# Where the value copies of layer B read from: SBUF row by row, or a copy in DRAM, two features at a time

## The chip, the cores and the metric

The kernel runs on one core of one Trainium2 chip. Its time is the device time of one execution in microseconds (us), without the host. The core has five engines that work side by side and meet only at semaphores: TensorE (PE, matmuls, with its weight loads shown apart as PEld), VectorE (DVE), ScalarE (ACT), GpSimd (POOL) and SyncE (SP), which here issues nearly all DMAs. Each engine runs its own list of instructions in order.

## The reference

The input x is 2048 rows of 512 features. Four layers run one after the other, A, B, A, B, each added to its input:

```
x = x + A(layernorm(x)); x = x + B(layernorm(x)); x = x + A(layernorm(x)); x = x + B(layernorm(x))
```

Layer A is a linear attention of 32 heads of 16 features: two softmaxes of each projected query and key, a sum over all rows that makes one small matrix per head, and a quotient. Every row of its second part needs the sum over all 2048 rows.

Layer B is an attention over a short window: row s looks at rows s, s-2, ..., s-14 of the same head, eight in all.

```
idx = pos[:, None] - (jnp.arange(8) * 2)[None, :]          # rows before 0 are masked
logits = einsum("bhsd,bhswd->bhsw", q, k[idx]) * Dh ** -0.5
attn = softmax(logits, axis=-1)
o = einsum("bhsw,bhswd->bhsd", attn, v[idx])
return o.reshape(B, S, D) @ wo
```

## The kernel before

**Blocks.** The 2048 rows are cut into four blocks of 512, b = 0 to 3, and L = 0 or 1 says which of the two A-B pairs is meant. A stage of a block is a closure registered under a name: `a1` to `a4` are layer A (keys and values, queries, denominators, output), `b1` projects queries, keys and values of layer B, `b2` makes the logits and the softmax, `b3` applies the weights to the values. `akv0` and `akv1` are the two places where the sum over all rows is turned into the matrices that `a3` and `a4` use.

**Two forms of layer B.** Seven of the eight blocks of layer B are elementwise: DVE multiplies shifted copies (`prod` at L1043, `pav` at L1105, four of each per block, a tile of 128 x 4096), and PE sums them with 0/1 matrices (`lgt` at L1050, `mo` at L1114). The eighth, L = 1 and b = 3 (`EST`), is done on PE with masked scores (`sc` at L1278, `b3_13.mo` at L1322, 128 short instructions each, four of them) and has its own way through DRAM (tile `Vs`, `vd`, the copies into `WA` and `Vx`, the copies `Qbd`).

**The values.** In an elementwise block the values V lie in one tile of 128 partitions by 4 x 528 elements: partition 4h + dl holds head h and feature dl of each of the four groups of features. The multiplication by the weights needs each feature dl on the partitions of all 32 heads and four window pairs g: `Vg[k]` with k = dl // 2 is a tile of [128, 2, 2112] in which partitions 32g to 32g + 31 hold the row of feature dl, shifted by 2g elements. The step `vrep(dl)` makes it with four DMAs, one for each g in the order 0, 2, 1, 3; each reads 32 partitions of V with a stride of four and writes 32 partitions, 4208 bytes a row. A block needs sixteen of them. `pav(q)` reads `Vg[q // 2]`, so the first two multiplications of a block need the first eight copies and the last two need the other eight.

**The order.** Nothing is scheduled on the chip. `_ORDER` lists all steps in the order in which they are recorded; an engine gets its own steps in that order. `_CHOICE` says for each flexible step (a copy out of PSUM, a normalization, a residual) whether ACT or DVE does it. `_SLOTS` says which of the fixed buffers each new tile takes: `ps` are the eight PSUM banks, `big` the eight large buffers in which `Ek`, `prod`, `pav`, `Vg`, `Qbd` and `Vx` follow one another, `med` and `t2` smaller ones. A step that takes a buffer waits for the last reader of its earlier tile. SP takes its DMAs in order too: a DMA that waits at the head of SP's list holds back all behind it, among them the transposes `xnT` (L473) that feed the next layer, the copies `Prho` (L855) of layer A and the stores of the result (L567).

**Steps that the prediction names.** `ev(2, c)` of `b1` are the four copies of V out of PSUM (tile `V`, L205 on ACT, L203 on DVE); `vhalo_in` (L989, POOL) fills the first sixteen columns of V; `vwr` (L997) writes V to DRAM and stands in the program before only behind an option that is off; `ld_raw1` are the two loads of raw key weights at the start (tile `wraw`, L349).

Of the kernel before, what the change touches and what calls it, by code (L numbers as in the profile page):

```python
# [19 lines left out]
H = 32  # L20
# [28 lines left out]
    "v_dram": (),  # L49
# [12 lines left out]
8 2e a d c 23 i i i 0 j 9 k j l i 2 i i i i 0 b o p i f 2 0 1m 1m 1o m n i i i i 1n 1m 1m 1p 1q 1m 1r o q r 1m t  # L62
4 z 1s s z i 3 1t 1u 21 z z 10 3 1t i7 1v 22 22 21 1 24 24 2p z 0 t u 13 11 15 1t 1t t 16 1w 1t 1y 12 12 12 12
1x x 1t 5 v w w 25 y 14 2f 2f 18 18 18 18 1z 2g 2c 17 6 19 18 1c 1d 39 2d 1b 1a 2d 22 22 1f 1f g 21 22 22 3a 3a
2c 2c 1f 2d 20 21 1f 22 2c 7 7 20 20 22 26 29 1g 1f 1k 39 3a 2d 2d 2d 2d 1i h 3b 2f 24 2i 1h 1e 29 1j 1l 2q 2h
27 2d 2n 3c 2o 2o 29 29 2a 39 2k 2k 3a 2k 2k 2n 2n 2n 2q 2o 2o 2r 3a 3a 2q 2q 2o 2o 2o 29 2y 2y 2l 2s 2k 2o 2z
2z 2z 2z 31 31 36 3c 33 24 36 36 28 36 2y 2y 2v 2v 2z 2v 37 36 2z 2z 2z 2f 2j 2u 2v 2b 2w 2b 2b 2b 2m 36 2m 36
2m 36 36 2m 39 3a 3b 3b 31 2v 2t 3a 31 32 4e 37 3c 34 35 39 3a 2x 2x 3c 2x 30 2x 38 38 36 38 38 3i 3c 3b 3c 3c
3c 7 3d 3e 3e 3j 3k 3k 3b 3k 3c 3l 5h 3m 3n 3m 3d 3e 3d 3l 5i 3o 3m 3e 3e 3l 3p 3m 3q 3r 3m 3m 5j 3d 3v 5i 3e 3e
3s 3e 20 20 20 20 3t 3m 5h 3u 5n 3m 3m 5m 3d 3e 7c 5h 5q 5o 5p 5r 5k 5i 3f 3g 3g 7 3f 3g 3g 5l 3m 5i 5i 7d 3w 3x  # L70
5i 5i 3z 5i 5i 3f 3f 7e 5i 5s 3g 3y 3g 40 41 7d 5w 42 7f 41 41 7f 41 5t 7f 3g 5v 3g 5u 5x 44 43 45 bd 43 43 46
43 47 5y 3f 43 47 48 90 5x 5x 4b e 49 4c 60 61 41 41 4a 41 41 3g 5x 5z 5z 4d 4g 4g 4h 5z 62 5z 4l 4l 4l 91 92 7d
7d 7g 63 4i 5z 91 4f 4n 4q 4q 4m 4q 63 66 67 64 65 7j 7i 7h 4l 7k 4r 93 4g 4g 4j 4w 4w 7l 7l 4o 4w 7o 68 4k 4q
4u 93 93 4t 4s 4f 7l 7p 7m 7n 4p 4v 7n 7l 7q 6p 6k 6k 4v 6k 7n 7n 91 91 6f 6g 7r 6n 6m 6k 6a 6a 4w 94 6l 7n 69
7r 7u 6o 7v 96 7t 97 4x 95 7s 7w 98 4x 4x 4x 6f 6c 6h 4y 4y 6a 6d 6b 6r 6r 99 6f 6i 6r 99 3h 99 99 9d 9e 3h 6f
6j 6a 6e 9a 9b 9c 9b 6r 9b 9b 83 7y 7y 84 9f 9b 8d 7z 6s 6s 6s 9f 9h 6s 6t 6t 88 89 9i 7y 6s 6t 4w 4x 83 83 6q
6q 7y 6q 85 88 4y 88 8b 83 9g 87 86 81 b2 9j 9k 88 8c 9m 9n 8f 9w 9x 82 9w 9w a1 6r 9z 69 6u 9w 80 6u 6v 8a 6u
6v 6x 6v 4w 6w 6q 6u 6v 6y 9m 4v 4z 4z 6z 4v 70 71 4z 4z 70 70 9y 72 7x 73 72 74 70 75 72 72 76 9o 9r 9r 50 51
8f 50 50 72 52 76 78 8e 8e 50 53 77 54 9r 9u 79 7a 9m 9p 7b 8f 9s 9t 55 8e 56 57 8f 55 58 55 55 59 8g 8g 8g 8e
a0 8g 57 57 a3 9r 5a 57 9v 9m 9q 5b a3 57 5b 8h 8h 5c b3 5e 5d 5f 5g 7x 9l a2 b0 b0 a3 b1 b1 b1 8g 8h b1 b3 b3  # L80
b6 b3 b7 bz c0 c0 a4 a4 a4 a3 a4 a5 a5 bz c0 c0 bz d3 b4 bz c0 c0 c0 c0 8f 8i b0 b1 a4 8i 8i 8i a5 as at b0 b1
b1 bx ap a2 b5 b1 ap 8j 8k 8j 8j 8l 8m 8j bx 8n 8o a3 a6 a2 a6 8p 8o 8o 8o bx aq aq aq aq by by by 8q 8t 8r 8s
as 8q a2 as as bx a6 a7 8q 8q a7 by 8u bz 8q a6 8u 8w 8y by by aw av 8v a7 8x a8 a7 aa ap ap a9 ab ac b8 b8 au
ac i7 ac ac by by bx b8 b8 ad aq aq af aq aq ag b9 bo c0 8z ah b8 bb bb ae ae ae ae ai be ax ae ai aj an c1 be
bc bb bc bc ak ax bc bb bc bc bc bc ac ac am ax ac ax ay al ac bg be bm bm ao bm bm bj bn bn bn bn bn bn ar ax
# [12 lines left out]
ig gs gs gs if if ig ig gp du if ig gs gt gt gt gt if gu ig if du du gu du dv ic c5 ic ic fd ih fe ih ih dy ig
ih ic dz ic dw ii ii fi ij gr gr gt ij ik ij ij fj fj ik il ga gu il in gs fl ii ij ij gv ii fj fj im ij ij ik
il ik fn fo gr gr il gw gx iq io iq iq gv gw gv gw gv gv ip iq iv dx dx fk fm fm gy gz h2 is gw gw ir it h2 iw  # L100
iu h0 it ix iw h3 h3 h4 h5 h6 h2 h1 h3 h7 h2 h5 h3 h8 h5 h5
# [4 lines left out]
    "0010110111100111111111000000100000100110011100000111011110010100000101010000100000000000111101011100"  # L106
    "1010010100001100100000000000000011111110000100001010100000000000000000010111001000001101000000000000"
    "1010000011111100000000000100010110011011010100101111000000001001000000010110010001000100011100100000"
    "00000000011111010000011100000000000000000000000001000011001000000000000000001100"
)  # L110


_SLOTS = {
    "med": (
        "0123456789abcdef346aff72ffc3105f92b4de6a7fd92b317ef99962c0517dbf2e3abf6925cd13e273a31dad901d74235cdb"
        "f72a94d35c017b9264acf31d08"
    ),
    "ps": (
        "0123124350123021456715604156734153267234701623047237452365001230210345672135304675261473045672350146"
        "1401230453013042567103651251741023452036714302310345031240230435406703203501467012012457245201240310"  # L120
        "3245602750235102563740130473024567142362047540123640760437034563745101021345067241301456701236204531"
# [8 lines left out]
        "333333301045234102"  # L130
    ),
    "pp": (
        "640620202020"
    ),
}


class _Fast:
# [804 lines left out]
    def s_b1(self, L, b):  # L943
# [55 lines left out]
        def vrep(dl):  # L999
            if dl == 0:  # L1000
                self.Vg[L, b] = {}
# [1099 lines left out]
```

## Time and profile before

| what | us |
|---|---|
| median of 3 runs (lowest, highest) | 328.83 (328.43, 328.86) |
| the profiled execution | 329.39 |
| its span, first to last instruction | 327.7 |
| PE / DVE / ACT busy in the span | 308.8 / 296.3 / 278.1 |

The span is what the trace covers; the profiled execution took 1.7 us more than it, and 0.6 us more than the median. Three engines are busy for 85 to 94% of the span. PE's figure holds overlaps, since the ends of matmuls are modelled. "issue" among the causes of a wait is time in which the engine waited for nothing that the profile shows. A row of the timeline gives start, length and count of merged instructions, and in brackets the idle time before them with what ended it. A row of the stretches gives for each engine its busy time and, in brackets, its instructions; then the granted PE clock, the share of time that the 16 DMA engines moved something (it can pass 1.0 by rounding), and GB/s.

### The profile page before, as it was taken

How to read it: one execution, taken by the hardware profiler on the slowest of the kernel's cores; microseconds unless marked ns; L12 is line 12 of the kernel's file. 1: busy time of each engine (PE TensorE's matmuls, PEld its weight loads, DVE VectorE, ACT ScalarE, POOL GpSimd, SP SyncE). 2: the span in 40 equal slices, each digit the busy share in tenths (PEclk: the TensorE clock that was granted, in tenths of full speed). 3: DMA queues.
4: the chain of work that ended last, by engine and by line, in shares of the span. 5: the costliest groups of instructions: out<-in, count | busy, mean ns of one | idle time of the engine just before them, and what ended most of it. 6: DMA issues, size and time to landing. Idle time of an engine off the chain costs nothing.

```text
span 327.7 us, 8877 instructions
## 1 busy us (share of the span) xinstructions
PE 308.8 (94%) x3542; PEld 153.5 (47%) x3574; DVE 296.3 (90%) x456; ACT 278.1 (85%) x640; POOL 39.1 (12%) x64
## 2 busy tenths in 40 slices
PE   7999999899999999999999999789999999986993
PEld 3644456444444454444444455543545444443441
DVE  6899995989999999999999999599898999999493
ACT  4999989999789977999999999799898866987360
POOL 6000000000020006000000000000040395210000
PEclk9999999999999999999999999999999999999799
DMA  7964300023677979679991200050588997549814
GB/s 203 341 162 90 108 2 4 2 68 81 144 172 140 132 149 158 108 131 131 145 121 28 40 0 4 4 141 9 145 147 121 192 136 131 135 83 176 158 67 137
DMA packets 45793, 36.41 MB, mean 111 GB/s; under 512 B 30832, under 2 KB 41136, under 8 KB 45744
## 3 DMA queue, kind: packets, MB, share of 16 engines
q1 hardware_dynamic: 45216, 35.75, 56.2%
q8 instruction: 30, 0.49, 0.7%
q14 instruction: 19, 0.16, 0.2%
q10 hardware_dynamic: 528, 0.02, 0.1%
HBM read 11.13 MB, written 3.25 MB: 44 GB/s over the span
## 4 chain that ended last, share of the span: by engine, by line
DVE 31%; ACT 31%; PE 18%; issue 12%; DMA 3%; SPq 2%; DVEq 0%; ACTq 0%
DVE prod L1043 6%; ACT Eq L729 5%; DVE pav L1105 5%; PE PS L543 5%; ACT sqd L563 5%; ACT Ek L622 4%; DVE x L556 4%; DVE Ek L674 3%; PE PS L951 3%; DVE xn L466 3%; ACT oT L205 2%; PE PS L1050 2%; DVE s L649 2%; ACT xn L468 2%; DMA wraw<-in_A_wqkv_dram 1%
## 5 line engine op out<-in xcount | busy, mean ns | idle before, releaser
L951 PE MATMUL PS<-xnT,WB 128*128 128x512 bf16 x336 | 76.7, 380 | 0.3 <-ACT K L205 0.2
L1105 DVE TENSOR_TENSOR pav<-PT,Vg 128x4096 bf16<-128x4096 bf16 (+1 forms) x29 | 63.3, 2219 | 0.6
L1043 DVE TENSOR_TENSOR prod<-QT,K 128x4096 bf16<-128x4096 bf16 x28 | 62.9, 2285 | 0.4 <-ACT QT L205 0.3
L951 PEld LDWEIGHTS <-WB 128*128 128x128 bf16 x336 | 37.3, 114 | 37.1 <-issue 4.2
L543 PEld LDWEIGHTS <-oT 128*128 128x128 bf16 x240 | 22.5, 98 | 31.3 <-issue 5.6
L729 ACT ACTIVATE Eq<-PS 128x512 bf16<-128x512 f32 x64 | 34.7, 624 | 0.0
L622 ACT ACTIVATE Ek<-PS 128x512 bf16<-128x512 f32 x64 | 33.9, 627 | 0.0
L563 ACT ACTIVATE sqd<-x 128x512 bf16<-128x512 bf16 x48 | 30.4, 633 | 2.1 <-DVE x L556 1.2
L721 PE MATMUL PS<-xnT,WA 128*128 128x512 bf16 x128 | 31.1, 380 | 0.2 <-ACT bs L870 0.2
L543 PE MATMUL PS<-WoB,oT 128*128 128x512 bf16 x105 | 27.7, 393 | 3.1 <-issue 2.9
L616 PE MATMUL PS<-WA,xnT 128*128 128x512 bf16 x124 | 29.9, 379 | 0.5 <-DVE x L556 0.2
L628 PE MATMUL PS<-WA,xnT 128*128 128x512 bf16 x122 | 29.9, 379 | 0.3
L543 PE MATMUL PS<-WoA,oT 128*128 128x512 bf16 x119 | 29.3, 380 | 0.8 <-DVE x L556 0.2
L556 DVE SCALAR_TENSOR_TENSOR x<-PS,x 128x512 bf16<-128x512 f32 x45 | 28.9, 684 | 0.3 <-PE PS L543 0.2
L205 ACT CAST oT<-PS 128x512 bf16<-128x512 f32 (+1 forms) x47 | 24.8, 595 | 3.8 <-PE PS L1114 3.5
L616 PEld LDWEIGHTS <-xnT 128*128 128x128 bf16 x128 | 12.3, 98 | 15.0 <-issue 0.6
L628 PEld LDWEIGHTS <-xnT 128*128 128x128 bf16 x128 | 12.3, 98 | 14.4
L205 ACT CAST V<-PS 128x512 bf16<-128x512 f32 x27 | 15.4, 591 | 4.1 <-PE PS L951 4.1
L674 DVE TENSOR_TENSOR Ek<-Ek,rk 128x4096 bf16<-128x4096 bf16 (+1 forms) x10 | 18.6, 1860 | 0.3 <-ACT rk L669 0.3
L721 PEld LDWEIGHTS <-WA 128*128 128x128 bf16 x128 | 11.7, 97 | 15.2 <-issue 2.0
L205 ACT CAST K<-PS 128x512 bf16<-128x512 f32 x30 | 17.4, 591 | 0.3 <-PE PS L951 0.3
L466 DVE TENSOR_SCALAR xn<-x,rstd,nmr 128x512 bf16<-128x512 bf16 x46 | 16.8, 408 | 0.6
(164 smaller groups left out, 496.9 us busy)
## 6 DMA issues: line engine op xcount, KB each, us to landing
Vg<-V SPq DMA_DIRECT2D x112, 131.5 KB, 4.8
Prho<-rd SPq DMA_DIRECT2D x8, 512.0 KB, 5.4
x<-in_A_x_dram SPq DMA_DIRECT2D x3, 512.0 KB, 5.8
WB<-in_B_wqkv_dram SPq DMA_DIRECT2D x3, 512.0 KB, 8.6
out_dram<-x SPq DMA_DIRECT2D x6, 256.0 KB, 2.3
wraw<-in_A_wqkv_dram SPq DMA_DIRECT2D x4, 256.0 KB, 5.4
vd<-Vs SPq DMA_DIRECT2D x2, 272.0 KB, 3.3
x<-in_A_x_dram SPq DMA_DIRECT2D x4, 128.0 KB, 3.9
```

The lines of the kernel that those rows point to most:

```text
L205: self.nc.scalar.copy(out=out, in_=in_)
L543: nc.tensor.matmul(y[:], lhsT=lh(t, c), rhs=Wo()[:, c, :], start=(c == 0), stop=(c == NB - 1 and not onpe))
L556: nc.vector.scalar_tensor_tensor(out=xb[:, t, :], in0=T[t][:], scalar=1.0, in1=xb[:, t, :], op0=ALU.mult, op1=ALU.add, **kw)
L563: nc.scalar.activation(out=sqd[:], in_=xb[:, t, :], func=ACT.Square, accum_out=T["ss"][:, t:t + 1])
L616: nc.tensor.matmul(pk[:], lhsT=xnT[:, t, k, :], rhs=self.WA[:, k, D:2 * D], start=(k == 0), stop=(k == NB - 1))
L622: nc.scalar.activation(out=T["E"][:, t, s, :], in_=T["k", t][:], func=ACT.Exp, scale=1.0 - 2.0 * s)
L628: nc.tensor.matmul(pv[:], lhsT=xnT[:, t, k, :], rhs=self.WA[:, k, 2 * D:3 * D], start=(k == 0), stop=(k == NB - 1))
L721: nc.tensor.matmul(pq[:], lhsT=self.WA[:, k, hb * P:(hb + 1) * P], rhs=xnT[:, :, k, :], start=(k == 0), stop=(k == NB - 1))
L729: nc.scalar.activation(out=self.Eq[L, b][s][:, :, hb, :], in_=T[hb][:].rearrange("p (t i) -> p t i", t=4), func=ACT.Exp, scale=1.0 - 2.0 * s)
L951: nc.tensor.matmul(pp[:], lhsT=self.WB[:, k, i * D + c:(i + 1) * D:NB], rhs=xnT[:, :, k, :], start=(k == 0), stop=(k == NB - 1))
L1043: nc.vector.tensor_tensor(out=pr[:], in0=QT[:, c:c + 1, :].to_broadcast([P, NW, TB]), in1=win, op=ALU.mult)
L1105: nc.vector.tensor_tensor(out=pv, in0=PT[:, :, lo:lo + n].unsqueeze(1).to_broadcast([P, NB, 2, n]), in1=vw, op=ALU.mult)
```

## The change

The seven elementwise blocks now write V to DRAM once (`vwr`, 128 rows of 2112 elements). `vrep` reads from there: one DMA fetches both features of a tile `Vg[k]` for one g, so that its 32 partitions get two rows of 4208 bytes. A block has one write and eight reads in place of sixteen copies. The steps are recorded as pairs, g = 0 and 2, then 1 and 3, for k = 0 and then k = 1. A read waits for the landing of the write. `_ORDER`, `_CHOICE` and `_SLOTS` are new throughout; the functions of all other steps are as they were.

```diff
-    "v_dram": (),
...
 _ORDER = """
-8 2e a d c 23 i i i 0 j 9 k j l i 2 i i i i 0 b o p i f 2 0 1m 1m 1o m n i i i i 1n 1m 1m 1p 1q 1m 1r o q r 1m t
...
+0 8 i i i i i 9 i i i i i i a j b 0 o 2 k j l m 0 t 2 p o q 0 t 1m 1m n i 1n i i 1o u r t v 3 3 1t bo 1m 1m 1q
...
-        def vrep(dl):
-            if dl == 0:
-                self.Vg[L, b] = {}
-            if dl % 2 == 0:
-                self.Vg[L, b][dl // 2] = self.big([2, NB * KVW], "Vg")
-            if (L, b) in _OPT["v_dram"]:
...
-            for g in (0, 2, 1, 3):
-                a = T["V"][dl:dl + 1, 0:1, 2 + 2 * g:3 + 2 * g]
-                src = bass.AP(a.tensor, a.offset, [[4 * a.ap[0][0], H], [1, VGW]])
-                nc.sync.dma_start(out=self.Vg[L, b][dl // 2][32 * g:32 * g + 32, dl % 2, 0:VGW], in_=src)
+        def vrep(k, gs):
+            if gs[0] == 0:
+                if k == 0:
+                    self.Vg[L, b] = {}
+                self.Vg[L, b][k] = self.big([2, NB * KVW], "Vg")
+            n = NB * KVW
+            for g in gs:
+                a = self.VD[L, b][2 * k:2 * k + 1, 2 + 2 * g:3 + 2 * g]
+                src = bass.AP(a.tensor, a.offset, [[4 * n, H], [n, 2], [1, VGW]])
+                nc.sync.dma_start(out=self.Vg[L, b][k][32 * g:32 * g + 32, :, 0:VGW], in_=src)
...
-        if (L, b) in _OPT["v_dram"]:
-            add(st + "v", "SP", vwr)
-        for dl in range(4):
-            add(st + "v", "SP", vrep, dl)
+        add(st + "v", "SP", vwr)
+        for k in range(2):
+            for gs in ((0, 2), (1, 3)):
+                add(st + "v", "SP", vrep, k, gs)
```

What the new lists move, as far as the prediction speaks of it. At the start SP issues x0(0), x0(1), raw1(0), x0(2), raw1(1), where it was x0(0), raw1(0), x0(1), raw1(1). At `akv0` the copy out of PSUM goes from DVE to ACT, and PE has one group of four query matmuls between the last sum and the transposes where it had two. In layer 1 the write of block 0 stands on SP before the last transpose of the next blocks' inputs; the write of block 1 stands among the first `Qbd` copies; the write of block 2 stands seven copies into the twelve that fill `WA` and `Vx`. At the end PE runs three of the four `b3_13.mo` in a row where it ran two, and DVE does its three `nrm` (L1349) before the first `pav` of the last block.

116 lines of the change are left out of this document (56 added, 60 removed).

## The prediction

> **What bounds the kernel now.** I read the page's busy times and its chain of waits first, then stretches of 20 us, because the shares are averages over unlike stages.
>
> ```profile
> PE 308.8 (94%) x3542; PEld 153.5 (47%) x3574; DVE 296.3 (90%) x456; ACT 278.1 (85%) x640; POOL 39.1 (12%) x64
> DVE 31%; ACT 31%; PE 18%; issue 12%; DMA 3%; SPq 2%; DVEq 0%; ACTq 0%
> ```
>
> ```profile
> 40.00:60.00 20.00, 19.41 (x474) 11.50 (x473) 15.88 (x29) 17.97 (x42) 0.00 (x0) 1.00 0.01 2
> 120.00:140.00 20.00, 19.86 (x136) 9.15 (x137) 19.79 (x16) 17.36 (x41) 5.88 (x5) 1.00 0.75 133
> 140.00:160.00 20.00, 19.81 (x136) 8.86 (x137) 19.47 (x15) 19.84 (x52) 0.15 (x1) 1.00 0.95 141
> 200.00:220.00 20.00, 16.87 (x429) 9.76 (x428) 16.21 (x33) 17.38 (x39) 0.00 (x0) 1.00 0.17 46
> 300.00:320.00 20.00, 17.22 (x276) 8.44 (x279) 14.34 (x18) 10.33 (x27) 0.00 (x0) 0.91 0.59 125
> ```
>
> The chain gives DMA 3% and SP's queue 2%: transfers hardly set the end. In the layer-B stages, from 120 to 160, DVE is busy 39.26 of 40 us: there only less DVE work could gain. The idle time is elsewhere: around `akv0` (40 to 60), around `akv1` (200 to 220) and at the end, where the clock falls too. How far was the old way of copying on a path of its own?
>
> ```profile
> L1012 SPq DMA_DIRECT2D Vg<-V x112: 467/592/1782, 91.9 to 304.1; - x112
> L1105 DVE TENSOR_TENSOR pav<-PT,Vg x29: 1215/2291/2348, 117.8 to 316.6; 128x4096 bf16<-128x4096 bf16 x27, 128x2048 bf16<-128x2048 bf16 x2
>   PEld L1114: 0.7, 2
> DMA to landing us min/median/max: 2.8/4.8/8.2
> ```
>
> This view of tile `Vg` ends with who waited for it: weight loads, 0.7 us in two waits, and DVE not at all. The first copies are issued at 91.9 and the first `pav` starts at 117.8. So nothing is to be gained on these waits; the new route can only keep them at nothing or add some.
>
> **The change part by part.** *Issue time on SP.* The 112 issues of median 0.592 us are 66 us of SP; 63 remain. SP is on the chain with 2%, most of it issues that wait for data, so the freed time is hidden behind DVE: I put 0, bounds -0.7 (one long issue of that row less on the path) to 0. If that cover went, it would be worth what follows for each block.
>
> *The route of one block.* These rows price it: twelve old copies in a row on SP, their rate, the load of `Prho`, which like the new reads goes from DRAM to SBUF, and, last, the landing of the four writes of `Vs`, which at 272 KB or less are the nearest to the new write of 541 KB.
>
> ```profile
> 256.85 9.02 SPq L1012 DMA_DIRECT2D Vg<-V  x12
> ```
>
> ```profile
> 86.50:92.00 5.50, 5.45 (x26) 2.64 (x26) 5.50 (x7) 3.13 (x6) 0.06 (x1) 1.00 1.02 235
> 256.80:266.00 9.20, 9.20 (x93) 4.19 (x95) 9.20 (x7) 7.55 (x17) 6.54 (x4) 1.00 1.06 162
> ```
>
> ```profile
> Vg<-V SPq DMA_DIRECT2D x112, 131.5 KB, 4.8
> ```
>
> ```profile
> DMA to landing us min/median/max: 2.4/2.7/4.0
> ```
>
> Copies alone moved 162 GB/s with the DMA engines full; the stretch with the `Prho` load moved 235. Eight reads move the same 2.1 MB as sixteen copies: 13.0 us at 162, 9.0 at 235. The write is 0.6 of issue and 2.7 (median) to 4.0 (longest) of landing; since it is twice the size, I take 4.0. From V to the last issue that gives 16 x 0.64 = 10.2 before (0.64 is the spacing, 0.592 plus the step to the next) and 0.6 + 4.0 + 8 x 0.64 = 9.7 after. But the first pair of features, which the first `pav` needs, was complete on SP after 8 x 0.64 = 5.1 and is now after 0.6 + 4.0 + 4 x 0.64 = 7.2: it comes 2.1 later. While SP waits for the write, everything behind it on SP waits too: reads of the same block, then transposes `xnT`.
>
> [...]
>
> *Where the route is on a path.* In layer 0 the V of a block is done 20 us or more before its first `pav`; 2.1 is hidden there. In layer 1 the new order gives blocks 0 and 1 little room. For block (1,0) I walk from the last sums of layer A (at 251.5 in the trace of before), with these durations:
>
> ```profile
> 251.53 0.30 ACT L450 ACTIVATE lnv<-q,eps_t 128x4 f32<-128x4 f32 x1 [0.23 <-DVE q L575]
> 252.57 1.52 ACT L468 ACTIVATE xn<-x,nmr,rstd 128x512 bf16<-128x512 bf16 x2 [0.51 <-DVE nmr L457]
> 255.21 0.59 ACT L205 CAST QT<-PS 128x512 bf16<-128x512 f32 x1
> 256.16 1.11 ACT L205 CAST QT<-PS 128x512 bf16<-128x512 f32 x2
> ```
>
> ```profile
> 252.38 0.16 DVE L457 SCALAR_TENSOR_TENSOR nmr<-sums,rstd 128x4 f32<-128x4 f32 x1
> 252.58 0.74 DVE L466 TENSOR_SCALAR xn<-x,rstd,nmr 128x512 bf16<-128x512 bf16 x2
> 253.23 8.89 DVE L1043 TENSOR_TENSOR prod<-QT,K 128x4096 bf16<-128x4096 bf16 x4
> 267.63 4.49 DVE L1105 TENSOR_TENSOR pav<-PT,Vg 128x4096 bf16<-128x4096 bf16 x2
> 272.05 0.68 DVE L1078 TENSOR_TENSOR PT<-E,rden 128x1024 bf16<-128x1024 bf16 x1
> ```
>
> ACT in the new order: 0.5 for the norm (251.53 to 252.07), one copy 0.48 (255.21 to 256.16 holds two), three `xn` 2.28 at 0.76, six copies 2.88 up to the last of V: 6.15. Write and landing 4.0: 10.2. Four reads issued: 12.1 (the fourth starts three spacings after the first). Landing 4.8 (the copies' median): 16.9. DVE in the meantime: norm 0.5 + 0.16, one `prod` 2.22, two `xn` 0.74, a copy 0.68, three `prod` 6.66, the mask 0.17, two `pav` of another block 4.44, `PT` 0.68: 16.25. So the first `pav` of (1,0) comes 0.6 late; with the shortest landings, 2.7 and 2.8, it has 2.7 to spare, with 8.2 for the reads it is 4.0 late. For (1,1), from that `pav`: DVE has four `pav`, one `prod` and a `PT`, 12.0; V is done after 2.2, written after 6.3, four reads issued after 8.2, landed after 13.0: 1.0 late, of which the first delay, if it occurs, has taken a part. What is late next is `mo` on PE and then the residual on DVE. Together I take +1.0, bounds 0 (the reads land at the rate of `Prho`) and +5 (both with long landings).
>
> *Start.* SP's first issues and the wait that depends on them:
>
> ```profile
> 1.26 0.42 SPq L349 DMA_DIRECT2D wraw<-in_A_wqkv_dram  x1
> 1.73 0.51 SPq L337 DMA_DIRECT2D x<-in_A_x_dram  x1
> ```
>
> ```profile
> PE PS L386 <- DMA wraw<-in_A_wqkv_dram: 1.0, 1, 1.0
> ```
>
> raw1(0) goes from second to third, one spacing of 0.47 later, and PE already waits 1.0 for it: +0.4, bounds 0 and 1.0 (it shares the DMA engines with one more x).
>
> *The two passes through `akv`.* Their waits:
>
> ```profile
> DVE kvT L203 <- PE PS L691: 1.0, 1, 1.0
> DVE ZM L776 <- PE PS L767: 1.5, 1, 1.5
> DVE ZM L776 <- ACT rS L743: 2.2, 1, 2.2
> ```
>
> ```profile
> 247.62 10.61 PE L951 MATMUL PS<-xnT,WB 128*128 128x512 bf16 x48
> ```
>
> At `akv0` one group of four matmuls less stands ahead of the transposes, 4 x 0.22 = 0.9 (10.61 by 48), and the copy goes to ACT. The wait of 1.0 is what this can shorten: -0.5, bounds -1.0 and 0. `akv1` keeps its waits.
>
> *Work moved between ACT and DVE.* Rows for one instruction each:
>
> ```profile
> L466 DVE TENSOR_SCALAR xn<-x,rstd,nmr 128x512 bf16<-128x512 bf16 x46 | 16.8, 408 | 0.6
> L205 ACT CAST K<-PS 128x512 bf16<-128x512 f32 x30 | 17.4, 591 | 0.3 <-PE PS L951 0.3
> L203 DVE CAST QT<-PS 128x512 bf16<-128x512 f32 x3 | 2.1, 688 | 0.0
> ```
>
> Of 512-wide copies DVE gains two and ACT loses two, two `xn` go from DVE to ACT, and one copy of 256 and half a transposed input go to ACT. DVE: 2 x 0.688 - 2 x 0.408 = +0.6, less up to 2 x 0.688 for the last two, -0.8. ACT: 2 x 0.76 - 2 x 0.591 = +0.3, plus up to 2 x 0.591, 1.5. I take +0.3 for the end, since DVE bounds and changes little; bounds -0.8 and 1.5. PE has the same 7149 instructions.
>
> *The end.* The largest single loss of the kernel lies here:
>
> ```profile
> 299.90:303.10 3.20, 0.65 (x4) 0.34 (x4) 2.81 (x5) 1.91 (x6) 0.00 (x0) 1.00 1.03 167
> 303.10:306.50 3.40, 3.40 (x9) 0.93 (x7) 1.94 (x1) 0.00 (x0) 0.00 (x0) 0.50 1.03 161
> ```
>
> ```profile
> 299.69 0.39 PE L1066 MATMUL PS<-E,indDen 128*128 128x512 bf16 x1
> 302.62 1.43 PE L543 MATMUL PS<-WoB,oT 128*128 128x512 bf16 x4 [2.55 <-issue]
> ```
>
> ```profile
> q8 instruction: 30, 0.49, 0.7%
> ```
>
> PE stands 2.55 for nothing but "issue", and then runs 3.4 at clock 0.50, which loses 1.7: about 4.25 together. It had just run the 256 short instructions of two `b3_13.mo` while the DMA engines were full (1.03). The instruction queue brings 0.49 MB in 30 packets, 16 KB each, 256 instructions of 64 bytes; I read the stop as the next packet coming late behind the copies, right at a packet's boundary (the program's 6577th PE instruction). In the new order that boundary lies behind three `mo` in a row, 384 short instructions: the same stop is due, and if the copies are still full then it can be longer. I take 0 for the difference, bounds -4.25 (the stop is gone) and +4.25 (it doubles).
>
> [...]
>
> *Sum.* 0 + 1.0 + 0.4 - 0.5 + 0.3 + 0 = +1.2. The profiled execution took 329.39, which is 0.56 above the median of 328.83: 329.39 + 1.2 = 330.6, and against the median 328.83 + 1.2 = 330.0.
>
> **The rivals.**
>
> R1, *the stop at the end is gone.* For it: the last eight transfers of a block come from DRAM, end 0.5 earlier on SP by the above, and are half as many, so the queue may be empty when PE asks for its next packet. Against it: one more burst of `mo`, and the same bytes in flight. 330.0 - 4.25 = 325.8.
>
> R2, *the reads land early*, at 235 GB/s and with a short write, so that no wait is added, the start costs nothing, and `akv0` and SP's issues give their whole bounds: -1.0 - 0.7 + 0.3 = -1.4: 327.4. For it: the old waits for `Vg` of 0.7 us in all, and SP's shorter list. Against it: it needs both landings below what I take.
>
> R3, *the write's round trip sets the pace of layer 1.* SP waits at the head of its list for a write in three blocks; each time the first pair is 2.1 late and the transposes or `Qbd` copies behind it as well. It decides once write and reads together take over 2 us longer than in the walk. 3 x 2.1 = 6.3: 335.1, slower. For it: the write of block 0 is ahead of a transpose, that of block 1 among the `Qbd` copies. Against it: DVE has multiplications of other blocks to go on with.
>
> R4, *the change does not do what it says*: reads no faster than copies (162 GB/s again, 13.0 us), with the write's 0.6 + 4.0 on top in the two blocks with little room, half of it covered: 2 x 2.3 = 4.6, against the 1.0 in the sum: 330.0 + 3.6 = 333.6.
>
> **How the numbers follow.** Forecast (329 to 331.5) 0.35; R1 0.25; R2 0.15; R3 0.12; R4 0.13. About 0.2%, 0.66 us, is what a measurement of this kernel can tell from no change. Faster holds R1 and nearly all of R2: 0.38. Same holds the forecast's lower edge, 329 to 329.5, and the rest of R2: 0.12. Slower holds the rest of the forecast, R3 and R4: 0.50. The predicted time is the likeliest's, 330.0. The range reaches from R1 with a little more, 325.3, to R3, 335.2; the forecast's own is 329 to 331.5.
>
> **What would show it right or wrong.** For the route: the write's landing between 2.7 and 4.0 us and the reads' near 4.8; a wait of DVE's `pav` at L1105 on a DMA of `Vg` at (1,0) and (1,1), near 0.6 and under 1.0 (R2: none; R3 and R4: some us, and transposes late too). For the start: PE's wait on `wraw` near 1.4. For `akv0`: no wait for the copy out of PSUM. For the end: an "issue" of about 2.5 us on PE followed by clock 0.50 between 295 and 315; without it R1 holds. The forecast is wrong if DVE's busy time changes by over 1.5 us, or if the new order has lost or closed idle time at a place that none of the steps names.

## The result, and the profile after

| kernel | median us (lowest to highest, runs) | ratio to before, 95% interval |
|---|---|---|
| before | 328.84 (327.18 to 328.97, 6) | 1 |
| changed | 343.53 (341.76 to 345.21, 6) | 1.0456 (1.0418 to 1.0494) |

The change costs 14.7 us by the medians and 4.6% by the ratio. The profiled execution has a span of 342.5 us against 327.7. Three lines of its page answer to those of before: the busy times, the chain of waits by engine, and the DMA issues.

```profile
PE 313.3 (91%) x3547; PEld 154.1 (45%) x3574; DVE 296.6 (87%) x453; ACT 279.5 (82%) x643; POOL 50.3 (15%) x64
PE 40%; ACT 25%; DVE 15%; DMA 12%; issue 5%; SPq 2%; DVEq 0%; ACTq 0%
...
Vg<-vd SPq DMA_DIRECT2D x56, 263.0 KB, 5.7
```

DVE does 0.3 us more and ACT 1.4: no work was added. DVE's share fell from 90% to 87%, and DMA stands in the chain with 12% where it had 3%: the loss is waiting. POOL is 11 us busier with the same 64 instructions; why comes up below, in layer 1. Where the time is lost shows when DVE's marks are set side by side: for `akv` (`ZM`), the multiplications `prod` and `pav`, first and last start (after, then before; the row of `pav` before stands in the prediction).

```profile
L775 DVE TENSOR_TENSOR ZM<-PS,maskH x4: 179/186/191, 54.5 to 212.1; 128x32 bf16<-128x32 bf16 x4
...
L1038 DVE TENSOR_TENSOR prod<-QT,K x28: 2278/2284/2323, 84.9 to 303.8; 128x4096 bf16<-128x4096 bf16 x28
...
L1100 DVE TENSOR_TENSOR pav<-PT,Vg x29: 1218/2285/2294, 118.9 to 330.1; 128x4096 bf16<-128x4096 bf16 x27, 128x2048 bf16<-128x2048 bf16 x2
```

```profile
L776 DVE TENSOR_TENSOR ZM<-PS,maskH x4: 180/186/190, 54.3 to 208.3; 128x32 bf16<-128x32 bf16 x4
...
L1043 DVE TENSOR_TENSOR prod<-QT,K x28: 2275/2284/2326, 84.0 to 290.9; 128x4096 bf16<-128x4096 bf16 x28
```

Up to the first `akv` the new kernel is 0.2 late, at the first `pav` 1.1, at the second `akv` 3.8, at the last `prod` (block (1,2)) 12.9, at the last `pav` 13.5. By the last `prod` the new order has done one `pav` more, so that 12.9 - 2.3 = 10.6 compares like with like. So some 3 us are lost in layer 0 behind the first `pav`, some 7 in layer 1 between the second `akv` and the last `prod`, and some 3 to 4 behind it, where the kernel before had its stop too. The waits of the changed kernel name the places (waiter, releaser: total, times, longest):

```profile
DVE pav L1100 <- DMA Vg<-vd: 7.9, 3, 4.8
DVE oB L1344 <- ACT rdB L1336: 7.7, 3, 4.8
...
PE PS L1109 <- DVE pav L1100: 5.5, 3, 2.3
...
PE PS L1317 <- issue: 4.5, 1, 4.5
...
PE PS L950 <- DMA xnT<-xn: 3.6, 1, 3.6
```

**The place in layer 0.** SP's timeline shows it (start, length, count of the merged issues); below it stand the last of these transposes in the kernel before, then one row of PE and one of DVE, then two stretches:

```profile
97.51 2.65 SPq L1007 DMA_DIRECT2D Vg<-vd  x6
101.28 4.95 SPq L472 DMA_TRANSPOSE xnT<-xn  x1
106.33 0.52 SPq L996 DMA_DIRECT2D vd<-V  x1
109.64 3.60 SPq L1007 DMA_DIRECT2D Vg<-vd  x8
114.24 6.57 SPq L472 DMA_TRANSPOSE xnT<-xn  x1
120.87 1.03 SPq L1007 DMA_DIRECT2D Vg<-vd  x2
```

```profile
115.72 2.83 SPq L473 DMA_TRANSPOSE xnT<-xn  x1
```

```profile
123.47 3.02 PE L950 MATMUL PS<-xnT,WB 128*128 128x512 bf16 x9 [3.60 <-DMA xnT<-xn]
```

```profile
126.02 4.49 DVE L1100 TENSOR_TENSOR pav<-PT,Vg 128x4096 bf16<-128x4096 bf16 x2 [2.60 <-DMA Vg<-vd]
```

```profile
110.00:120.00 10.00, 9.87 (x69) 4.75 (x68) 9.60 (x12) 8.64 (x21) 3.32 (x4) 1.00 0.99 225
120.00:130.00 10.00, 6.53 (x23) 2.90 (x23) 7.40 (x4) 6.11 (x9) 0.00 (x0) 0.83 0.55 100
```

Eight reads leave SP in 3.6 us, one every 0.45: 263 KB by 0.45 us is 584 GB/s, and the DMA engines, full (0.99), move 225. SP's issue of the transpose behind them takes 6.57 us (2.83 in the kernel before). Two things are late behind it: PE stands 3.60 us for the transposed input, and DVE 2.60 for the last reads of block (0,1), which SP could only issue at 120.87. The clock of 0.83 in the second stretch is 10 x 0.17 / 0.5 = 3.4 us at half speed, behind PE's idle time.

**The place in layer 1.** POOL, SP and DVE, then POOL in the kernel before:

```profile
260.74 4.81 POOL L992 COPY vh<-V 128x64 bf16<-128x64 bf16 x1 [7.37 <-ACT V L204]
265.61 5.07 POOL L988 COPY V<-vh 128x64 bf16<-128x64 bf16 x1
270.62 2.65 POOL L1150 MEMSET WA<- 128x3072 bf16 x1
273.21 3.51 POOL L1143 MEMSET Qbd<- 128x4096 bf16 x1
```

```profile
264.89 3.86 SPq L1007 DMA_DIRECT2D Vg<-vd  x8
276.75 2.63 SPq L1221 DMA_DIRECT2D Qbd<-Qs  x4
279.48 0.52 SPq L996 DMA_DIRECT2D vd<-V  x1
280.05 1.90 SPq L1221 DMA_DIRECT2D Qbd<-Qs  x3
282.58 2.66 SPq L1007 DMA_DIRECT2D Vg<-vd  x6
```

```profile
258.74 6.68 DVE L1038 TENSOR_TENSOR prod<-QT,K 128x4096 bf16<-128x4096 bf16 x3
...
265.50 4.48 DVE L1038 TENSOR_TENSOR prod<-QT,K 128x4096 bf16<-128x4096 bf16 x2
269.90 0.68 DVE L1073 TENSOR_TENSOR PT<-E,rden 128x1024 bf16<-128x1024 bf16 x1
...
289.62 4.50 DVE L1100 TENSOR_TENSOR pav<-PT,Vg 128x4096 bf16<-128x4096 bf16 x2 [4.82 <-DMA Vg<-vd]
```

```profile
259.40 2.82 POOL L993 COPY vh<-V 128x64 bf16<-128x64 bf16 x1 [10.69 <-ACT V L205]
262.28 0.24 POOL L989 COPY V<-vh 128x64 bf16<-128x64 bf16 x1
```

Followed back from the wait, link by link: DVE stands 4.82 us for the reads of block (1,1); SP issued them at 282.58, behind the landing of the write of 279.48; that write stood behind Qbd copies that waited on SP from 269 to 276.75; these waited for POOL's fill of Qbd, which ended at 276.7; and POOL was late by two small copies of 4.81 and 5.07 us, of a kind that took 0.24 in the last row. Each of the two ends where a run of DVE multiplications ends (265.4 and 270.6), so it is DVE that seems to have held the copies, by my reading of these rows; the experiment with these copies on ACT, below, tests what they cost. In the kernel before, the first eight copies of block (1,1) stood on SP ahead of all Qbd copies, so that POOL could not hold them up.

**The end.** The stop for "issue" is there again, now one instruction into the third `b3_13.mo`, and longer, 4.49 us against 2.55:

```profile
316.61 0.24 PE L1317 MATMUL PS<-WA,et 128*32 128x68 bf16 x2 [4.49 <-issue]
```

### The profile page after: what moved, and what is told of

Read it like the earlier page. It is cut to its first block, busy times and chain, and to the rows that moved or that the text cites. A ratio compares the mean times of both kernels' runs of the same rounds, so it can differ in the third digit from the quotient of the medians.

```text
span 342.5 us, 8806 instructions
## 1 busy us (share of the span) xinstructions
PE 313.3 (91%) x3547; PEld 154.1 (45%) x3574; DVE 296.6 (87%) x453; ACT 279.5 (82%) x643; POOL 50.3 (15%) x64
## 4 chain that ended last, share of the span: by engine, by line
PE 40%; ACT 25%; DVE 15%; DMA 12%; issue 5%; SPq 2%; DVEq 0%; ACTq 0%
PE PS L950 9%; PE PS L542 7%; PE PS L627 5%; DMA xnT<-xn 5%; PE PS L615 5%; ACT sqd L562 4%; DMA Vg<-vd 4%; ACT Ek L621 4%; PE PS L720 4%; DVE prod L1038 4%; ACT Eq L728 4%; ACT oT L204 3%; DVE x L555 2%; DMA wraw<-in_A_wqkv_dram 2%; PE PS L1045 2%
## 5 line engine op out<-in xcount | busy, mean ns | idle before, releaser
L950 PE MATMUL PS<-xnT,WB 128*128 128x512 bf16 x336 | 79.8, 391 | 3.9 <-DMA xnT<-xn 3.6
L1100 DVE TENSOR_TENSOR pav<-PT,Vg 128x4096 bf16<-128x4096 bf16 (+1 forms) x29 | 63.0, 2214 | 10.6 <-DMA Vg<-vd 7.9
L204 ACT CAST oT<-PS 128x512 bf16<-128x512 f32 (+1 forms) x51 | 27.6, 592 | 7.6 <-PE PS L1109 7.4
L542 PE MATMUL PS<-WoB,oT 128*128 128x512 bf16 x106 | 28.8, 399 | 0.6 <-issue 0.4
L1109 PE MATMUL PS<-pav,indAV 128*32 128x512 bf16 (+1 forms) x232 | 15.1, 382 | 5.8 <-DVE pav L1100 5.5
L720 PEld LDWEIGHTS <-WA 128*128 128x128 bf16 x128 | 11.6, 98 | 13.4 <-issue 0.3
```

The lines of the kernel that those rows point to most:

```text
L204: self.nc.scalar.copy(out=out, in_=in_)
L542: nc.tensor.matmul(y[:], lhsT=lh(t, c), rhs=Wo()[:, c, :], start=(c == 0), stop=(c == NB - 1 and not onpe))
L720: nc.tensor.matmul(pq[:], lhsT=self.WA[:, k, hb * P:(hb + 1) * P], rhs=xnT[:, :, k, :], start=(k == 0), stop=(k == NB - 1))
L950: nc.tensor.matmul(pp[:], lhsT=self.WB[:, k, i * D + c:(i + 1) * D:NB], rhs=xnT[:, :, k, :], start=(k == 0), stop=(k == NB - 1))
L1100: nc.vector.tensor_tensor(out=pv, in0=PT[:, :, lo:lo + n].unsqueeze(1).to_broadcast([P, NB, 2, n]), in1=vw, op=ALU.mult)
```

## The experiments

All times are medians; "before" was run again beside each group and stood at 328.8, 329.5, 329.2 and 329.35 us, so the ratios are what to compare. Where the intervals of two ratios overlap, the two times are not told apart. In the order lists below, `b1_01v` is the part of stage `b1` that deals with V, for L = 0 and b = 1; `vrep(k, gs)` issues two reads and `tr` a transpose.

| run | us | ratio to before (95%) |
|---|---|---|
| old order, new route | 333.23 | 1.0116 (1.0063 to 1.0169) |
| new order, old route | 349.79 | 1.0639 (1.0616 to 1.0662) |
| write of (1,1) ahead of the Qbd copies | 340.45 | 1.0346 (1.0321 to 1.0370) |
| last reads of (0,1) ahead of the transpose | 345.53 | 1.0479 (1.0431 to 1.0528) |
| before, boundary shifted by 126 | 327.82 | 0.9951 (0.9922 to 0.9979) |
| changed, boundary shifted by 64 | 338.36 | 1.0268 (1.0224 to 1.0313) |
| transpose behind four reads, not eight | 343.67 | 1.0407 (1.0371 to 1.0443) |
| old order, new route, boundary shifted | 328.71 | 0.9982 (0.9956 to 1.0008) |
| second pair of (0,0) read last | 340.20 | 1.0322 (1.0289 to 1.0355) |
| three mended together | 333.15 | 1.0117 (1.0083 to 1.0151) |
| halo copies on ACT | 340.41 | 1.0356 (1.0308 to 1.0404) |
| three mended, halo copies on ACT | 334.53 | 1.0181 (1.0145 to 1.0217) |

**Route and order apart.** First the old lists with the new route. Since a `pav` now needs both features of its `Vg[k]`, all four reads of a tile stand where its first old copies stood:

```diff
         def vrep(dl):
             if dl == 0:
                 self.Vg[L, b] = {}
+                vwr()
+            k = dl // 2
...
-            for g in (0, 2, 1, 3):
-                a = T["V"][dl:dl + 1, 0:1, 2 + 2 * g:3 + 2 * g]
...
+            for g in (0, 2, 1, 3) if dl % 2 == 0 else ():
+                a = self.VD[L, b][2 * k:2 * k + 1, 2 + 2 * g:3 + 2 * g]
+                src = bass.AP(a.tensor, a.offset, [[4 * n, H], [n, 2], [1, VGW]])
```

> The kernel before with its order, choices and slots, only the route new: one write of V and eight reads per block, all four reads of a tile Vg[k] issued where its first old copy stood. Theory P (the loss comes from places in the new order: SP held by POOL's fill of Qbd ahead of the write of block (1,1), a transpose stuck behind eight reads ahead of the last reads of block (0,1), the tail): the route alone costs little here, 328 to 332 us, waits of pav for Vg under 3 us in all. Theory R (the round trip through DRAM itself, wherever it stands): 335 us or more, with waits of pav for Vg in several blocks.

333.23 us, 4.4 over the kernel before: between the two theories. The waits settle it:

```profile
PE PS L543 <- issue: 5.2, 1, 5.2
...
DVE pav L1103 <- DMA Vg<-vd: 1.0, 1, 1.0
```

DVE waits 1.0 us for `Vg` in the whole kernel. What grew is the stop for "issue" at the end, 5.2 us where it was 2.55. Then the converse, the new lists with copies out of SBUF:

```diff
         def vwr():
-            self.VD[L, b] = self.dram.tile([P, NB * KVW], BF16, name="vd%d%d" % (L, b))
-            nc.sync.dma_start(out=self.VD[L, b][:], in_=T["V"][:].rearrange("p c t -> p (c t)"))
+            pass
...
+            for d in range(2):
+                for g in gs:
+                    a = T["V"][2 * k + d:2 * k + d + 1, 0:1, 2 + 2 * g:3 + 2 * g]
+                    src = bass.AP(a.tensor, a.offset, [[4 * a.ap[0][0], H], [1, VGW]])
```

> The changed kernel with its new order, only the route old: no write, sixteen copies of 131 KB out of SBUF in the places of the eight reads. P: part of the loss stays, because in block (1,1) the copies still stand behind Qbd copies that wait for POOL, and the tail is the same: 334 to 340 us; the transposes in layer 0 are issued in 2 to 4 us again, not 5 to 6.6, since 131 KB in 0.64 us builds up less of a backlog. R: with the round trip gone the time comes back to 329 to 331 us.

349.79 us, above what either theory gave. Taking the round trip away does not bring the time back: the new order is 6.3 us slower still.

```profile
DVE pav L1099 <- DMA Vg<-V: 10.2, 5, 3.9
DVE K L202 <- DMA Vg<-V: 10.1, 1, 10.1
```

A copy of K waits 10.1 us for copies out of V; I read this as a buffer that the new `_SLOTS` hands on as soon as V is written to DRAM and that sixteen copies hold longer; this was not tried. So the 6.3 us are not the price of the round trip alone. The transposes are issued in 4.4, 5.0 and 4.2 us at the places of the three long ones, still over the 2 to 4 expected.

**Layer 1: what stands ahead of the write.** Only the order of SP's steps changes (`qsc` are the Qbd copies; the first line stands for four):

```diff
-b1_13q.qsc(0, 0) to qsc(3, 0)
 b1_11v.vwr()
-b1_13q.qsc(4, 0) to qsc(6, 0)
 b1_11v.vrep(0, (0, 2))
 b1_11v.vrep(0, (1, 3))
 b1_11v.vrep(1, (0, 2))
+b1_13q.qsc(0, 0) to qsc(6, 0)
```

> The changed kernel, but on SP the seven Qbd copies that stand before or among the write and the first six reads of block (1,1) come after them; nothing else moves. P: the write is issued near 272 us instead of 279.5, the wait of 4.82 us of DVE's pav for Vg in (1,1) is gone, and the kernel gains 3 to 5 us: 338.5 to 340.5. R: the reads are late all the same (round trip and rate): gain under 1 us.

340.45 us, 3.1 less. The views are SP's timeline and one row of the DMAs issued from 271 to 279 us (size, time to landing):

```profile
272.19 0.34 SPq L994 DMA_DIRECT2D vd<-V  x1
278.96 2.65 SPq L1005 DMA_DIRECT2D Vg<-vd  x6
```

```profile
vd<-V SPq DMA_DIRECT2D x1, 528.0 KB, 6.6
```

The write goes at 272.19, and the wait of 4.82 before the first `pav` of (1,1) is 0.48. The reads follow only at 278.96, right behind the landing of the write, which took 6.6 us where it took 3.0 in the changed kernel: the eight reads of block (1,0), issued from 265 on, were still moving ahead of it (DVE's first `pav` of that block waited for them until 272.75). So here the round trip does hold SP, made long by a backlog. 3.08 us of wait appear at the block's second pair, whose reads are still among the Qbd copies, and DVE's waits for `Vg` are 8.2 us in all, no less than before this edit (7.9). DVE's next `prod` behind the block starts at 297.76 in place of 299.37, 1.6 us earlier; in this trace the low clock around 295 us also lasts 3.4 us in place of 6.8, which is worth another 1.7.

Then the cause on POOL, in the changed kernel:

```diff
         def vhalo_in():
             vtile()
+            if (L, b) == (1, 1):
+                nc.scalar.copy(out=T["V"][:, :, 0:16], in_=self.vh[L, b - 1][:])
+                return
...
         def vhalo_out():
+            if (L, b) == (1, 0):
+                nc.scalar.copy(out=self.vh[L, b][:], in_=T["V"][:, :, TB:KVW])
+                return
```

> The changed kernel, but the two copies of 128 x 64 elements that hand the last columns of V from block (1,0) to (1,1) are made by ACT instead of POOL, where they took 4.81 and 5.07 us while DVE ran its multiplications back to back. Theory G (they hold up POOL's fills of WA and Qbd, which hold up SP and the write of (1,1) behind it): on ACT each takes under 0.5 us, the first Qbd copy starts 4 to 8 us before 276.7, DVE's wait of 4.82 us for Vg falls below 1.5, gain 2 to 5 us: 338.5 to 341.5. Rival (POOL's fill of Qbd waits for its buffer's last reader anyway): the first Qbd copy starts within 1 us of where it was, no gain.

340.41 us, 3.1 less; the first Qbd copy starts at 268.89, 7.9 earlier, and the waits for `Vg` fall from 7.9 to 3.9, the longest 2.6 (1.5 was expected). So POOL did hold SP there. The size of the gain is less certain: the four runs reach from 338.49 (mean clock 0.989, the run of the trace) to 342.71 (0.970). In that trace PE stands 3.6 us for `xnT` in layer 0 as in the changed kernel, and the clock stays at 1.00 behind it, where it fell to 0.50 for 3.4 us; that is up to 1.7 us which this edit did not bring.

```profile
PE PS L950 <- DMA xnT<-xn: 3.6, 1, 3.6
```

```profile
120.00:130.00 10.00, 6.80 (x44) 3.42 (x47) 7.42 (x4) 6.97 (x11) 0.00 (x0) 1.00 0.48 95
```

POOL's timeline:

```profile
261.74 3.51 POOL L1149 MEMSET Qbd<- 128x4096 bf16 x1 [7.54 <-PE PS L1051]
265.69 4.99 POOL L976 COPY K<-K 128x64 bf16<-128x64 bf16 x1 [0.44 <-ACT K L204]
```

The fill takes 3.51 us, like the fills of `Qbd` that lie inside DVE's multiplications in the two kernels (from 273.21 in the changed one, from 262.45 in the one before), while the next copy takes 4.99. Why such a copy is held up and a fill is not, these rows do not show.

**Layer 0: who waits behind the backlog.** Three orders of SP. First the last two reads of (0,1) ahead of the transpose:

```diff
 b1_01v.vrep(1, (0, 2))
 b1_00v.vrep(1, (1, 3))
+b1_01v.vrep(1, (1, 3))
 a4_03o.tr()
-b1_01v.vrep(1, (1, 3))
```

> The changed kernel, but the last two reads of block (0,1) stand on SP before the transpose of block 3's input, which took 6.57 us to issue, instead of behind it. P: DVE's wait of 2.6 us for Vg there is gone; the transpose comes some 1 us later and PE waits that much longer for it; gain 1 to 2.6 us: 341 to 342.5. R: no change (within 0.7), since the reads' own rate sets when they land.

345.53 us, 2.0 more by the medians, with intervals that overlap: no gain, and a miss.

```profile
114.57 8.14 SPq L470 DMA_TRANSPOSE xnT<-xn  x1
```

```profile
PE PS L948 <- DMA xnT<-xn: 5.4, 1, 5.4
```

DVE was not what counted there: with ten reads ahead the transpose is issued in 8.14 us, and PE waits 5.4 instead of 3.6, with a longer stretch of low clock behind it (the slice of the page around 124 us has a granted clock of 6 tenths, in the changed kernel 8). So the transpose next, ahead of four of the reads (here and in the next experiment the tile of the pair that moves takes its buffer where it did, so that `_SLOTS` still holds):

```diff
 b1_01v.vrep(0, (1, 3))
-b1_01v.vrep(1, (0, 2))
-b1_00v.vrep(1, (1, 3))
 a4_03o.tr()
+b1_00v.vrep(1, (1, 3))
+b1_01v.vrep(1, (0, 2))
 b1_01v.vrep(1, (1, 3))
```

> The changed kernel, but in layer 0 the transpose of block 3's input stands on SP behind four reads instead of eight; the other four and the last two of block (0,1) come after it. Theory Q (the transpose waits behind the backlog of reads, PE waits for it 3.6 us, and the clock falls to 0.50 for 3.4 us behind that idle time): its issue takes under 4.5 us instead of 6.57, PE's wait for xnT and the fall of the clock near 124 are gone, DVE waits about 1 us for Vg instead of 2.6; gain 2.5 to 4.5 us: 339 to 341. Rival (the transpose itself is slow at this place, and the reads then come later by as much): within 1 us of 343.5.

343.67 us, no gain beyond the overlap of the intervals: the rival's number. The transpose is issued in 2.91 us and PE's wait for it is gone, both as expected, but the reads behind it are late by as much:

```profile
126.06 13.55 DVE L1101 TENSOR_TENSOR pav<-PT,Vg 128x4096 bf16<-128x4096 bf16 x6 [3.27 <-DMA Vg<-vd]
```

Both point to the bytes: 14 reads and two writes, 14 x 263 + 2 x 528 KB = 4.7 MB, are asked for from 94.8 to 114, where the kernel before had asked for twenty copies, 2.6 MB. Four of the reads are the second pair of block (0,0), and all `pav` of that block come after the four of (0,1). With these reads put last:

```diff
 b1_00v.vrep(0, (1, 3))
-b1_00v.vrep(1, (0, 2))
 a4_02o.tr()
 b1_01v.vwr()
...
 b1_01v.vrep(1, (0, 2))
-b1_00v.vrep(1, (1, 3))
 a4_03o.tr()
 b1_01v.vrep(1, (1, 3))
+b1_00v.vrep(1, (0, 2))
+b1_00v.vrep(1, (1, 3))
```

> The changed kernel, but in layer 0 the four reads of block 0 for its second pair of features, which no pav needs before 130 us, come after all reads of block 1 and after the transpose, instead of before them. Theory Q2 (the DMA engines are behind in this stretch because 14 reads and two writes, 4.7 MB, are asked for before the transpose at 114; what is not needed soon stands ahead of what is): both the PE wait for xnT with the fall of the clock near 124 and DVE's wait of 2.6 us for Vg go; gain 3 to 5 us: 338.5 to 340.5. Rival (the stretch is bound by the DMA engines whatever the order): the wait moves to another pav again, within 1 us of 343.5.

340.20 us, 3.3 less, as expected. The longest issue of any transpose is now 3.98 us (the row of the tile: shortest, median, longest in ns), PE's wait for `xnT` is 0.5 us, and the waits for `Vg` are 2.4 us in all:

```profile
L470 SPq DMA_TRANSPOSE xnT<-xn x11: 1435/2018/3977, 22.1 to 257.1; - x11
```

**The end: instruction packets.** Three warming matmuls at the start give way to many small ones, so that every packet's boundary moves:

```diff
+        self.pad = 66
         def warm():
...
+            if self.pad:
+                m = min(self.pad, 22)
+                self.pad -= m
+                for _ in range(m):
+                    nc.tensor.matmul(self.warm_ps[0:32, 0:68], lhsT=self.kvT[:, 0:32], rhs=self.kvT[:, 0:68], start=True, stop=True)
+                return
             nc.tensor.matmul(self.warm_ps[:], lhsT=self.kvT[:, 0:P], rhs=self.kvT[:], start=True, stop=True)
```

In the kernel before:

> The kernel before, with 126 more PE instructions at its start: three of the warming matmuls (512 columns, about 0.44 us each) are replaced by 66 small ones with their weight loads (about 0.02 us each). It moves every instruction packet's boundary 126 instructions forward in the program, so that the one that lay behind the two b3_13.mo in a row falls between them. Theory F (PE ran out of instructions at that boundary): the stop of 2.55 us for issue near 300 and the clock of 0.50 behind it go, gain 3 to 4.3 us: 324.5 to 326. Rival (the stop has another cause, a place in the program or the DMA load alone): 328.8 within 0.7, with the stop where it was.

327.82 beside 329.5: 1.7 us less, about half of what was expected, and between the numbers of the two theories. It is the only run of the table whose interval lies below 1. The stop near 300 is gone and the clock stays at 1.00; a shorter one, without a fall of the clock, comes later.

```profile
310.48 0.83 PE L1373 MATMUL PS<-ident,oB 128*32 128x128 bf16 x19 [1.10 <-issue]
```

```profile
300.00:310.00 10.00, 9.36 (x327) 5.86 (x320) 9.03 (x10) 6.72 (x21) 0.00 (x0) 1.00 0.97 166
310.00:320.00 10.00, 9.52 (x91) 4.31 (x91) 7.94 (x16) 4.78 (x10) 0.00 (x0) 1.00 0.43 148
```

DMA is as full as it was in the stop before (0.97), so full DMA engines alone do not make the stop. The small matmuls cost some 1 us at the start: the first three `prod` on the chain begin at 85.18, where it was 84.05.

The changed kernel with `self.pad = 34`, which makes 64 more instructions:

> The changed kernel, with 64 more PE instructions at its start by the same means (two warming matmuls for 34 small ones): the boundary moves into the middle of the second of the three b3_13.mo. F: no packet is then made of short instructions alone, the stop of 4.49 us at L1317 and the clock of 0.50 behind it go or fall below 1 us, gain 4 to 8 us: 335.5 to 339.5. Rival: within 1 us of 343.5.

338.36 us, 5.2 less, as expected; a stop of 1.3 us is left, where under 1 was expected. In this trace, too, the clock stays at 1.00 behind PE's wait for `xnT` in layer 0 (3.7 us), so that up to 1.7 of the 5.2 us need not be the stop's.

The old order with the new route, with `self.pad = 66`:

> The old order with the new route (first experiment), with the same 126 more PE instructions at the start. F says that its 4.4 us over the kernel before are the same stop, there 5.18 us with 6.8 us of clock 0.50 instead of 2.55 and 3.4, because reads load the DMA engines more than copies: without it the route alone costs nothing, 324.5 to 326.5, within 1 us of the kernel before with the same padding. Rival: the loss is the route's elsewhere, and 328 or more remain.

328.71 us: within 1 us of the kernel before with the same shift (0.9 more, with intervals that overlap), but over 326.5 and, taken alone, the rival's number. Here a stop remains, with 3.4 us of low clock behind it:

```profile
305.46 0.19 PE L1327 MATMUL PS<-Vx,et 128*32 128x68 bf16 x1 [2.53 <-issue]
```

Where these stops lie shows the boundary better than the times do. Count PE's matmuls and weight loads in order of time (the traces of the two kernels themselves lack some 30 of 7148 records and are left out). Without a shift the stop stands before number 6576 to 6578; in the shifted runs it stands before 6834 (changed kernel, by 64), 6832 (old order with the new route, by 126) and 7088 (kernel before, by 126): 256 or 512 further each time, at different places of the program. That excludes a place in the program as the cause. The instruction queue brings 30 packets and 0.49 MB in the changed kernel as in the one before, 16 KB a packet; the steps of 256 agree with a packet of 256 instructions, which makes 64 bytes for each, an estimate from these numbers.

How long it lasts goes with the route. Seven runs with reads and no shift have 4.49 to 5.8 us. The two with copies have 2.55 (old order) and 2.52 (new order; the profile puts it down to DVE's `oB`, but in the shifted run of the changed kernel the third `mo` runs before that `oB`). The DMA engines are full in the stops of the two kernels themselves; they move 265 GB/s in that of the changed kernel (share 1.02) and 168 in that of the kernel before (1.03). Why the stop is longer with more of this traffic is not shown.

**Together.** The order of SP in layer 1, that in layer 0, and the shift by 64:

> The changed kernel with three edits together: Qbd copies behind the write of block (1,1), the second pair of block (0,0) read last, and 64 more PE instructions at the start. Theory P+F+Q2 (three separate places hold nearly the whole loss): 343.5 - 3.1 - 4 - 5.2 = 331, between 329.5 and 333. Rival (the places cover for each other: mending one lets the next wait show): 334 or more.

333.15 us, 0.15 above the upper edge of the expectation. By the medians 10.4 us are won back, where the three alone give 3.1 + 3.3 + 5.2 = 11.6; by the ratios 11.1, where they give 3.6 + 4.4 + 6.2 = 14.2. So the three cover for each other by 1 to 3 us.

Then with the halo copies on ACT besides:

> The three mended places and, besides, the two halo copies of V from block (1,0) to (1,1) on ACT. If POOL's 4.8 and 5.1 us still hold up something that is not yet mended (the fills of Qbd, with the last pair of reads and the K halo behind them), it gains another 1 to 3 us: 330 to 332. If the write of (1,1), already ahead of the Qbd copies here, was all that POOL held up, the time stays at 333 within 0.7, and what remains to the kernel before is the waits for Vg in layer 1 (7.0 us in three) that the order leaves.

334.53 us, 1.4 more and outside both expectations: no gain from POOL shows, once the write no longer stands behind the fills.

What is left is more than the 4 us to the kernel before. The mended kernel has its boundary shifted; like is the kernel before with its own shift, 327.82 us, and to that 5.3 us are left. That is as much as the two edits of SP's order won on top of the shift, 338.36 - 333.15 = 5.2. DVE still waits 7.0 us for `Vg` in three places (7.8 us in six with the halo copies on ACT). One price is visible: the write of (1,1), behind the eight reads of (1,0), takes 7.3 us to land in the mended kernel. Which of the remaining steps of the order makes the rest was not tried.

## Why the prediction was wrong

The sign was the one held likeliest, the size was not: 330.0 was forecast, 343.53 is above the range. That the sign came out right is partly luck: it was forecast from landings in layer 1 (+1.0), and the loss came mostly from what stands ahead of what on SP and from the stop at the end, which the sum had at 0.

*Work and start: right.* DVE +0.3 and ACT +1.4 in busy time, and 0.2 us late at the first `akv` where the terms +0.4 and -0.5 stood.

*Prices of the route: nearly right.* The write lands in a median of 3.2 us (2.7 to 4.0 were given), reads in 5.7 (4.8 taken, 8.2 the bound; longest 8.8). With reads in flight the DMA engines moved 225 GB/s, between the bounds of 162 and 235, so R4 falls, and R2 with the landings. The median hides the case that mattered: behind eight reads the write took 6.6 and 7.3 us, over the bound of 4.0. The walk also left out the write's own 0.6 us of issue, which the price before it has.

*The spacing of the issues: wrong, and this mattered.* I gave a read the 0.64 us of an old copy; SP needs 0.45. Copies of 131.5 KB every 0.64 us asked for 205 GB/s, where 162 were moved; reads ask for 584. The freed issue time was counted as worth 0, when it builds a queue in which the next transpose waits.

*"In layer 0 ... 2.1 is hidden there": the step that failed first.* It looked at V and `pav` alone. The bytes asked for ahead of a transpose were not counted, and the transpose was named only as something behind a waiting write. The order of the reads there is worth 3.3 us. I also took it that the first `pav` had always needed two features. With the old copies it needed only its own four (the kernel before reads `Vg[q // 2][:, q % 2]`), so that by the prices of the prediction it comes 7.2 - 4 x 0.64 = 4.6 us later and not 2.1.

*Block (1,0): a little short.* 0.6 late was forecast. DVE waited 1.73 us before its first `pav`. The profile names PE, but the page's chain has the fourth read landing at 266.44 + 5.75 = 272.19, 0.1 before that `pav` started, so that the reads alone would have made it 1.6 late. Before its third `pav` DVE waited 0.5 for `Vg`.

*Block (1,1), "V is done after 2.2, written after 6.3": the step that failed most.* The write was issued 279.48 - 272.31 = 7.2 us after that `pav` and landed after 10.2. The front part said that this write stands among the Qbd copies; the walk then left out what those wait for, POOL, whose queue was not looked at. 1.0 late was forecast, 4.82 measured, and PE and the clock lost more behind it (PE stood 2.33 us for `pav`, and the clock was 0.50 for 6.8 us from 295.2). R3 had this place and the right sign, but its mechanism, a round trip of 2.1 us three times, was not what decided: SP was held by another engine, not by a landing. Only once that was mended did a landing hold SP, the 6.6 us of the write.

*The end: the stop foreseen, the place and the size off.* PE stopped for "issue" again, as said, and R1 falls. But the prediction put the boundary behind three `mo`, 384 short instructions; it lies behind two again and one instruction more, so a longer burst is not why the stop is longer. The term 0 measures 4.49 - 2.55 = 1.9 of idle time, and more low clock (6.8 us of it against 3.4); the bound of +4.25 held it. The term left out that reads load the DMA engines more than copies (265 GB/s in the stop against 168). The experiments with shifted boundaries bear out that the stop is bound to an instruction number, in steps of 256; that a packet comes late there is still my reading, and no run shows the packet itself.

*What the runs show of the change as a whole.* Route alone +4.4 us, some 3 of it by the longer stop at the end (2.63 us more, and 4.3 in place of 3.4 us of work at half clock), and 0.9 with the boundary shifted in both kernels; order alone +21; both +14.7. So the route costs mostly at the boundary. The rest of the price is the new order's, and only with the route that it was made for is it as good as 343.5. Two places of it are shown, by experiments: the backlog ahead of a transpose in layer 0, and the write of (1,1) behind POOL's fill. Some 5 us of it stay open.

## What to carry to other kernels

Fewer and larger DMAs freed the issuing queue here (56 reads, one every 0.45 us, for 112 copies), but what it then issued was a backlog (584 GB/s asked for, 225 moved): count the bytes asked for ahead of each transfer that somebody soon waits for, and issue first what is needed first. Before a DMA is moved on a queue that issues in order, as SP's list does here, ask of each instruction that will stand ahead of it which engine it waits for, and follow that engine's queue too, the idle one above all. Before an edit is credited with a gain, see whether the clock fell at the same places in both traces. The wait for "issue" on PE moved when the program was shifted by 64 or 126 instructions, which brought 5.2 us in the changed kernel (up to 1.7 of them not the stop's), 4.5 with the old order and the new route and 1.7 in the kernel before; stops of 1.1 to 2.53 us stayed.

## What the runs showed of the hardware

A copy of 128 x 64 elements on POOL took 0.24 us where DVE was between two runs of multiplications (kernel before, 262.28), and up to 5.07 us while DVE multiplied two tiles back to back (changed kernel, 265.61); it ended with DVE's run. Fills of 128 x 4096 elements on POOL took 3.51 us while DVE multiplied, in both kernels. The issue of a transpose on SP took 1.4 to 8.1 us; that of block 3 in layer 0 took 2.91 behind four reads, 6.57 behind eight and 8.14 behind ten.

The granted clock fell to 0.50 behind PE idle times of 2.53 us (old order, new route, shifted) and 2.55 (kernel before), not behind one of 1.10 (kernel before, shifted). But the length of the gap does not decide alone: behind 3.60 us at the same place the clock fell in the changed kernel and not in the run with the halo copies on ACT, nor behind 3.7 us in the shifted run. In the changed kernel's trace the falls begin at 124.5, 295.2 and 315.7 us, 170.7 and 20.5 apart, which is 50 and 6 times 3.41, and they last 3.41 or 6.83 us; so in this trace the changes of the clock lie on a grid of 3.41 us. That the place of a gap on this grid decides whether the clock falls is my estimate from these few gaps; no run tests it.
